# First MoE layer norm: the variance on all partitions, and its Newton steps on 256 columns

## The chip, the cores and the metric

One core of one Trainium2 chip runs the whole program. The metric is device time in microseconds (us) for one execution; a median over runs is given. The engines are TensorE (PE, with its weight loads as PEld), VectorE (DVE), ScalarE (ACT) and GpSimd (POOL); SyncE (SP) issues most transfers.

## The reference, cut to what matters

Three layers follow each other: attention with two sparse masks (4 batches of 576 tokens, 8 heads of 64), a first MoE layer on the 2304 tokens of 512 features, and a second MoE layer with eight experts. The change concerns the layer norm at the head of the first MoE:

```
mu = mean(x); var = mean((x - mu) ** 2)           # over the 512 features of a token
xn = (x - mu) / sqrt(var + 1e-6) * g_ln
x  = x + relu(xn @ w_ch1) @ w_ch2                 # 512 -> 2048 -> 512
```

## The kernel before, in words

Tokens are cut into nine chunks of 256 (CT); features lie on the partitions, so a chunk x is a tile of 128 x 4 x 256 and a mean over features is a product with `mean_w`, a 128 x 128 matrix of 1/512. Such a product leaves the mean of every token on all 128 partitions. The factor 1/sqrt(var) isn't applied to x but to the result of the second product: `post` multiplies the accumulated output by it, so it isn't needed before the chunk's last turn.

The first MoE runs in turns t. A turn is one pair (chunk c, block f of 128 hidden features): `mm1` makes 12 products into ps_h, ScalarE and VectorE split h = relu(ps_h) into a high and a low part (L641, L642), and one turn later `mm2` adds 12 products into acc. Chunks 0 and 1 are interleaved in turns 0 to 31 (chunk 0 ends in turn 28, chunk 1 in turn 31), because the weights are still being prepared there: each of 32 pieces goes through VectorE (L455), ScalarE (L461, L462), VectorE (L467, the join), ScalarE (L481, the cast to the high part) and GpSimd (L484, the low part). Attention of the next batch runs between them in turns 8 to 26 (ps_sc, sm, ps_pt, ps_o). Chunks 2 to 8 follow one by one.

Layer norm of chunks 0 and 1, by functions placed at turns through `when(t, ...)`: `ln_2` takes the mean and subtracts it, `ln_3` squares, `ln_4` takes the variance and the inverse root, `ln_back` adds the mean again, and `ln_5` brings the root into its final form. ln_4 is at turns 3 and 9, ln_5 at turns 27 and 30. In ln_4, each of two blocks of 128 tokens takes four products with one column of mean_w, the squares being the weights, so that the variance of a token stands on the token's own partition, in two columns; an integer guess and three Newton steps (three VectorE instructions each) follow on 128 x 2. ln_5 scales the identity by the two columns (dg), multiplies it by mean_w into ps_rs, and ScalarE copies the 128 x 256 result to rsb. Chunks 2 to 8 already use `ln_w`, which works on 128 x 256 after one product.

Instructions are written in this order, but a scheduler puts each engine's queue in order beforehand: of the instructions that are ready by its own clock it takes the one written first, so that one written late can stand early in a queue. Instructions marked with `keep` (those of the weight pieces) stay in order among themselves. On the chip each queue runs in its fixed order.

Buffers: pools with a tag have as many buffers as `bufs`; ln_p has one each of the tags sq, mu, rs and s, and a new tile of a tag waits for the last reader of the old one. side_r gives one of two PSUM buffers in this stage.

Of the kernel before, what the change touches and what calls it, by code (L numbers as in the profile page):

```python
# [9 lines left out]
F32 = mybir.dt.float32  # L10
# [3 lines left out]
I32 = mybir.dt.int32  # L14
U32 = mybir.dt.uint32
AF = mybir.ActivationFunctionType
ALU = mybir.AluOpType
# [6 lines left out]
DM, DF = 512, 2048  # L24
# [4 lines left out]
CT = 256  # L29
NCHUNK = NT // CT  # L30
TT = 128
NTT = CT // TT
# [40 lines left out]
def attention_moe_moe(ctx: ExitStack, tc: tile.TileContext, q, k, v, g_ln, w_ch1, w_ch2, w_gate, w_local, w1, w2, out):  # L73
# [15 lines left out]
    pe, act, dve = Pin(nc.tensor), Pin(nc.scalar), Pin(nc.vector)  # L89
# [14 lines left out]
    ident = iw[:, 0, NE + 1:NE + 129]  # L104
    make_identity(nc, ident)
    pool.tensor_copy(iw[:, 1, NE + 1:NE + 129], ident)
    mean_w = cst.tile([128, 128], F32, name="mean_w")
# [46 lines left out]
    rt_p = ctx.enter_context(tc.tile_pool(name="rt_p", bufs=1))  # L154
    ps_acc = ctx.enter_context(tc.tile_pool(name="ps_acc", bufs=1, space=PSUM))
    ps_m = ctx.enter_context(tc.tile_pool(name="ps_m", bufs=2, space=PSUM))

    at_x = ExitStack()
    at_p = at_x.enter_context(tc.tile_pool(name="at_p", bufs=1))
# [19 lines left out]
    def side_r(shape, name):  # L179
        return ps_s["r"].tile(shape, F32, tag="s", name=name)  # L180
# [373 lines left out]
    def ln_3(c):  # L554
# [11 lines left out]
            pool.tensor_tensor(s_, s_, sq, op=ALU.add)  # L566
        lns[c] = s_

    def ln_4(c):

        s_ = lns[c]
        ps = side_r([128, NTT], "ps_var")
        for j in range(NTT):
            for d in range(4):
                pe.matmul(ps[:, j:j + 1], s_[:, d, TT * j:TT * j + TT], mean_w[:, 0:1], start=(d == 0), stop=(d == 3))
        va = ln_p.tile([128, 3, NTT], F32, tag="va", bufs=2, name="va")
        va, rs, t = (va[:, i, :] for i in range(3))
        dve.tensor_scalar(va, ps, 1e-6, None, op0=ALU.add)
        dve.tensor_single_scalar(rs.bitcast(I32), va.bitcast(I32), 1, op=ALU.logical_shift_right)
        dve.tensor_scalar(rs.bitcast(I32), rs.bitcast(I32), -1.0, float(0x5F3759DF), op0=ALU.mult, op1=ALU.add)  # L580
        for _ in range(3):
            dve.tensor_tensor(t, rs, rs, op=ALU.mult)
            dve.scalar_tensor_tensor(t, t, -0.5, va, op0=ALU.mult, op1=ALU.mult)
            dve.scalar_tensor_tensor(rs, t, 1.5, rs, op0=ALU.add, op1=ALU.mult)
        lns[c] = rs

    newton = {}

    def ln_w(c, k):

        if k == 0:
            ps = side_r([128, CT], "ps_var")
            pe.matmul(ps, mean_w, lns[c], start=True, stop=True)
            va, t, rs = (ln_p.tile([128, CT], F32, tag=g, name=n) for g, n in (("sq", "va"), ("mu", "nt"), ("rs", "rsb")))
            newton[c] = va, t
            lns[c] = rs
            dve.tensor_scalar(va, ps, 1e-6, None, op0=ALU.add)
            dve.tensor_single_scalar(rs.bitcast(I32), va.bitcast(I32), 1, op=ALU.logical_shift_right)
            dve.tensor_scalar(rs.bitcast(I32), rs.bitcast(I32), -1.0, float(0x5F3759DF), op0=ALU.mult, op1=ALU.add)
        else:  # L600
            va, t = newton[c]
            rs = lns[c]
            dve.tensor_tensor(t, rs, rs, op=ALU.mult)
            dve.scalar_tensor_tensor(t, t, -0.5, va, op0=ALU.mult, op1=ALU.mult)
            dve.scalar_tensor_tensor(rs, t, 1.5, rs, op0=ALU.add, op1=ALU.mult)

    def ln_5(c):
        rs = lns[c]
        dg = ln_p.tile([128, NTT, TT], F32, tag="sq", name="dg")
        for j in range(NTT):  # L610
            dve.tensor_scalar(dg[:, j, :], ident, rs[:, j:j + 1], float(DM), op0=ALU.mult, op1=ALU.mult)
        ps = side_r([128, CT], "ps_rs")
        pe.matmul(ps, mean_w, dg.rearrange("p j t -> p (j t)"), start=True, stop=True)
        rsb = ln_p.tile([128, CT], F32, tag="rs", name="rsb")
        act.copy(rsb, ps)
        lns[c] = rsb

    def ln_split(c):
        x = xts[c]
# [347 lines left out]
    for n in range(2):  # L967
        i = n * (NE + 129)
# [49 lines left out]
    def when(t, fn, *args):  # L1018
        at.setdefault(t, []).append(lambda: fn(*args))
# [7 lines left out]
    for c in range(NCHUNK):  # L1027
        first = order.index((c, 0))
        if c > 1:
            for t, fn in zip(LN_AT if c > 2 else (-3, -2, -1), (ln_1, ln_2, ln_3)):  # L1030
                when(first + t, fn, c)
            when(first - 1, ln_split, c)
            when(first - 1, ln_back, c)
            for i, t in enumerate(LN_W):
                when(first + t, ln_w, c, i)
        else:
            when(last[c] - 1, ln_5, c)
        if c + 1 < NCHUNK:
            t = last[max(c, 1)] + (5 if c == 1 else 0)
            for i, (fn, *args) in zip(RT[c > 1], [(rt_rows, c, 0, 0), (rt_rows, c, 0, 1), (rt_rows, c, 1, 0), (rt_rows, c, 1, 1), (rt_soft, c), (rt_scan, c), (rt_list, c), (rt_hot, c), (rt_sum, c)]):  # L1040
                when(t + i, fn, *args)
# [24 lines left out]
    for t, (c, f) in enumerate(order):  # L1066
        need = (2 * f + 4 + 2 * (f == 14) if f < 15 else len(turns)) + WA if t <= last[0] else 0
        while nw[0] < min(len(turns), max(need, W_START + int(WR * t))):
            weights_next()
        if f == 0 and c > 1:  # L1070
            products()
            if c == 2:
                side_pools(False, s=4)
            elif c == 6:
                at_x.close()
                side_pools(False, s=3, r=1)
            elif c == NCHUNK - 1:
                load_turn(0)
                m2_p = ctx.enter_context(tc.tile_pool(name="m2_p", bufs=1))
        mm1(c, f)  # L1080
        while late:
            post(late.pop(), 1)
        for kind in ORDER:
            if kind == "T":
                while len(fifo["t"]) > (TL if plan.get(t) or plan.get(t + 1) else 0):
                    do("t")
            elif kind == "B":
                carry_ += plan.get(t, 0)
                while carry_:
                    carry_ -= 1  # L1090
                    prepped = pos[0] < len(steps) and steps[pos[0]][0] == "prep"
                    begin([])
                    if prepped:
                        break
            elif kind == "X":
                do_all("x")
            elif kind == "A":
                for fn in at.get(t, []):
                    fn()
            elif kind == "M":  # L1100
                products()
                pend.append((c, f))
            elif kind == "N":
                normed = take("n", 9)
                for p in [p for un in normed for p in st_norm(*un)]:
                    p()
            elif kind == "O":
                if len(fifo["o"]) > 1 or not (fifo["x"] or fifo["n"] or fifo["t"] or plan.get(t + 1) or plan.get(t + 2)):
                    do_all("o")
            else:  # L1110
                fifo["t"] += normed
# [514 lines left out]
```

## Time and profile before

| | |
|---|---|
| median of 3 runs | 873.81 us (873.71 to 874.35) |
| profiled execution | 874.09 us, span 872.0 us |
| TensorE busy | 846.9 us, 97% of the span |
| VectorE, ScalarE, GpSimd busy | 460.3, 353.9, 171.6 us |
| mean granted clock of TensorE | 0.993 |

Times in the rows below count from the span's start. A busy TensorE is modelled from matmuls that overlap, so its gaps show better in the weight loads (PEld). The number in brackets behind a row is how long the engine sat idle before it and what ended that.

### The profile page before, as it was taken

To read this page: it belongs to the slowest core of one execution; us is meant where nothing else is said; L and a number is where in the kernel's file an instruction comes from. 1 tells how busy PE (TensorE), PEld (TensorE's weight loads), DVE (VectorE), ACT (ScalarE), POOL (GpSimd) and SP (SyncE) were. 2 spreads that over 40 slices of the span, in tenths; PEclk is the share of its full clock that TensorE was granted. 3 is DMA by queue.
4 is the path that set the end of the run, shared out by engine and by line. 5 is a ranking of instruction groups with operands and counts; after the bars stand their busy time and mean duration, and the time that the engine had idled before them with its cause. 6 is when DMAs were issued, how large, how long until landed. Compare 5 with 4: busy or idle time off the path is not lost. (4 is left out here: it accounts for less than half of the span.)

```text
span 872.0 us, 18871 instructions
## 1 busy us (share of the span) xinstructions
PE 846.9 (97%) x7123; PEld 753.2 (86%) x7130; DVE 460.3 (53%) x1542; ACT 353.9 (41%) x857; POOL 171.6 (20%) x257
## 2 busy tenths in 40 slices
PE   9999999999999999999999999999999999999994
PEld 5688888889999999999999999999788868778773
DVE  4876765457656546566555464585815151121641
ACT  3787876542455233354211222242113252222551
POOL 2245542240120120120111212010032122121111
PEclk9999999999999999999999999999999999999998
DMA  9936352211211102210000000501266275454830
GB/s 181 263 122 207 100 150 70 52 32 53 66 44 45 50 9 59 52 32 15 26 2 26 1 26 1 194 30 45 89 240 235 70 257 207 147 186 170 300 121 23
DMA packets 96547, 87.16 MB, mean 100 GB/s; under 512 B 67379, under 2 KB 75575, under 8 KB 96441
## 3 DMA queue, kind: packets, MB, share of 16 engines
q1 hardware_dynamic: 89256, 69.61, 26.6%
q0 software_dynamic: 3552, 11.11, 3.7%
q10 hardware_dynamic: 3632, 5.09, 1.6%
q8 instruction: 59, 0.97, 0.4%
q14 instruction: 48, 0.39, 0.1%
HBM read 76.27 MB, written 9.97 MB: 99 GB/s over the span
## 5 line engine op out<-in xcount | busy, mean ns | idle before, releaser
L655 PE MATMUL acc<-h,w 128*128 128x256 f32 x1728 | 246.2, 290 | 3.2 <-DVE h L642 1.8
L639 PE MATMUL ps_h<-xc,w 128*128 128x256 f32 x1728 | 236.8, 286 | 0.0
L655 PEld LDWEIGHTS acc<-h,w 128*128 128x128 f32 x1728 | 218.5, 191 | 9.6 <-DVE h L642 3.1
L639 PEld LDWEIGHTS ps_h<-xc,w 128*128 128x128 f32 x1728 | 219.3, 192 | 1.7
L641 ACT ACTIVATE h<-ps_h 128x256 fp32r<-128x256 f32 x144 | 55.7, 388 | 214.4 <-PE ps_h L639 200.0
L642 DVE SCALAR_TENSOR_TENSOR h<-ps_h,h 128x256 fp32r<-128x256 f32 x144 | 60.4, 420 | 100.8 <-ACT h L641 100.4
L87 PE MATMUL ps_y<-wx,ht 128*128 128x512 f32 x336 | 83.6, 398 | 0.0
L484 POOL TENSOR_TENSOR w<-stg,w 128x128 fp32r<-128x128 f32 x128 | 62.9, 523 | 104.1 <-ACT w L481 54.5
L87 PE MATMUL ps_h<-wx,xs 128*128 128x512 f32 x336 | 81.0, 397 | 0.0
L87 PEld LDWEIGHTS ps_h<-wx,xs 128*128 128x128 f32 x336 | 62.7, 188 | 14.8
L87 PEld LDWEIGHTS ps_y<-wx,ht 128*128 128x128 f32 x336 | 61.1, 188 | 11.9 <-issue 0.2
L896 DVE TENSOR_TENSOR xs<-ps_tx,xs 128x512 fp32r<-128x512 f32 x14 | 9.7, 692 | 63.5 <-ACTq L1369 47.9
L1461 ACT ACTIVATE h<-ps_h 128x512 f32<-128x512 f32 x28 | 15.2, 595 | 56.4 <-PE ps_h L87 56.4
L785 DVE TENSOR_TENSOR wx<-raw,wx 128x1024 fp32r<-128x1024 f32 x32 | 37.3, 1217 | 1.3 <-ACT wx L782 1.3
L461 ACT ACTIVATE stg<-stg 128x512 f16<-128x512 f32 x27 | 37.1, 1374 | 0.3 <-DVE stg L455 0.3
L1475 DVE TENSOR_TENSOR ht<-ps_th,ht 128x512 fp32r<-128x512 f32 x28 | 18.5, 685 | 32.9 <-ACT ht L1474 32.8
L1499 POOL DMA_INDIRECT out_dram<-y,idx x14 | 17.8, 1270 | 89.7 <-ACT y L1498 81.0
L782 ACT CAST wx<-raw 128x1024 fp32r<-128x1024 f32 x32 | 31.8, 1059 | 5.6 <-PE acc L655 4.1
L355 ACT ACTIVATE sm<-sm,st 128x54 f32<-128x54 f32 (+1 forms) x80 | 27.6, 348 | 12.7 <-DVE st L343 12.6
L1474 ACT CAST ht<-ps_th 128x512 fp32r<-128x512 f32 x28 | 15.1, 589 | 36.2 <-PE ps_th L87 36.2
L467 DVE SCALAR_TENSOR_TENSOR stg<-stg 128x512 int32<-128x512 int32 x27 | 18.9, 700 | 16.4 <-ACT stg L462 15.6
L875 POOL DMA_INDIRECT xg<-xrows,idx x15 | 16.1, 1073 | 54.1 <-issue 33.1
(397 smaller groups left out, 1181.5 us busy)
## 6 DMA issues: line engine op xcount, KB each, us to landing
raws<-in_moe_w_dram SPq DMA_DIRECT2D x20, 1024.0 KB
stg<-in_moe_w_ch_dram SPq DMA_DIRECT2D x32, 512.0 KB
raw<-in_moe_w_dram SPq DMA_DIRECT2D x16, 1024.0 KB
xrows<-row ACTq DMA_DIRECT2D x9, 520.0 KB
qnat<-in_q_dram SPq DMA_DIRECT2D x48, 72.0 KB
knat<-in_k_dram SPq DMA_DIRECT2D x48, 72.0 KB
v<-in_v_dram SPq DMA_DIRECT2D x24, 72.0 KB
v<-in_v_dram SPq DMA_DIRECT2D x72, 18.0 KB
```

The lines of the kernel that those rows point to most:

```text
L87: return lambda *args, **kw: tc.keep_in_program_order(fn(*args, **kw))
L355: act.activation(sm[0:m, i, :], (ps if mode else sm)[0:m, i, :], AF.Exp, bias=st[0:m, 0, i:i + 1], scale=-1.0, **({} if mode else dict(acc ...
L461: keep(act.activation(t.bitcast(F16)[..., 1], f32(t[..., 1]), AF.Copy, scale=2.0 ** -112))
L467: keep(dve.scalar_tensor_tensor(t[..., 1], t[..., 1], 3, t[..., 0], op0=ALU.logical_shift_left, op1=ALU.bitwise_or))
L484: keep(pool.tensor_tensor(o, x, f32(h), op=ALU.subtract))
L639: pe.matmul(ps, w[:, a, d, o:o + 128], xcs[c][:, b_, d, :], start=(i == 0), stop=(i == 11))
L641: act.activation(h[:, 0, :], ps, AF.Relu)
L642: dve.scalar_tensor_tensor(h[:, 1, :], ps, 0.0, f32(h[:, 0, :]), op0=ALU.max, op1=ALU.subtract)
L655: pe.matmul(accs[c][d // 2][:, d % 2, :], w[:, a, f % 2, d * 128:(d + 1) * 128], h[:, b_, :], start=(f == 0 and (a, b_) == (0, 0) and d % ...
L782: act.copy(wx[i][:, 0, :], raw[i // 2][:, i % 2, :])
L785: dve.tensor_tensor(wx[i][:, 1, :], raw[i // 2][:, i % 2, :], f32(wx[i][:, 0, :]), op=ALU.subtract)
L1475: dve.tensor_tensor(s_[1][:, 4 * g:4 * g + 4, :], ps, f32(s_[0][:, 4 * g:4 * g + 4, :]), op=ALU.subtract)
```

## The change: what it does

For chunks 0 and 1 the variance is taken as the mean is: four products of 256 columns with mean_w as weights, which leaves it on all partitions as 128 x 256. Only the addition of 1e-6 stays in ln_4. The integer guess and the three Newton steps work on 128 x 256 and are placed at the four turns 24 to 27 (chunk 0) and 27 to 30 (chunk 1). The scaling of the identity, the product into ps_rs and ScalarE's copy go. Chunk 1 gets a buffer of its own for va, in a pool that is closed after turn 31, and a tag of its own, rs1, for the result. `ln_w` of the later chunks calls the same helpers and does what it did.

```diff
+    va_x = ExitStack()
+    va_p = va_x.enter_context(tc.tile_pool(name="va_p", bufs=1, side="right"))
...
     def ln_4(c):
-        s_ = lns[c]
-        ps = side_r([128, NTT], "ps_var")
-        for j in range(NTT):
-            for d in range(4):
-                pe.matmul(ps[:, j:j + 1], s_[:, d, TT * j:TT * j + TT], mean_w[:, 0:1], start=(d == 0), stop=(d == 3))
-        va = ln_p.tile([128, 3, NTT], F32, tag="va", bufs=2, name="va")
-        va, rs, t = (va[:, i, :] for i in range(3))
+        ps = side_r([128, CT], "ps_var")
+        for d in range(4):
+            pe.matmul(ps, mean_w, lns[c][:, d, :], start=(d == 0), stop=(d == 3))
+        va = (va_p if c else ln_p).tile([128, CT], F32, tag="sq", name="va")
         dve.tensor_scalar(va, ps, 1e-6, None, op0=ALU.add)
+        newton[c] = va, None
+
+    def ln_5(c, k):
+        if k == 0:
+            newton[c] = va, t = newton[c][0], ln_p.tile([128, CT], F32, tag="mu", name="nt")
+            lns[c] = ln_p.tile([128, CT], F32, tag=("rs", "rs1")[c], name="rsb")
+            seed(c)
+        else:
+            newton_step(c)
+
+    def seed(c):
+        va, rs = newton[c][0], lns[c]
         dve.tensor_single_scalar(rs.bitcast(I32), va.bitcast(I32), 1, op=ALU.logical_shift_right)
         dve.tensor_scalar(rs.bitcast(I32), rs.bitcast(I32), -1.0, float(0x5F3759DF), op0=ALU.mult, op1=ALU.add)
-        for _ in range(3):
-            dve.tensor_tensor(t, rs, rs, op=ALU.mult)
-            dve.scalar_tensor_tensor(t, t, -0.5, va, op0=ALU.mult, op1=ALU.mult)
-            dve.scalar_tensor_tensor(rs, t, 1.5, rs, op0=ALU.add, op1=ALU.mult)
-        lns[c] = rs
+
+    def newton_step(c):
+        (va, t), rs = newton[c], lns[c]
+        dve.tensor_tensor(t, rs, rs, op=ALU.mult)
+        dve.scalar_tensor_tensor(t, t, -0.5, va, op0=ALU.mult, op1=ALU.mult)
+        dve.scalar_tensor_tensor(rs, t, 1.5, rs, op0=ALU.add, op1=ALU.mult)
...
-    def ln_5(c):
-        rs = lns[c]
-        dg = ln_p.tile([128, NTT, TT], F32, tag="sq", name="dg")
-        for j in range(NTT):
-            dve.tensor_scalar(dg[:, j, :], ident, rs[:, j:j + 1], float(DM), op0=ALU.mult, op1=ALU.mult)
-        ps = side_r([128, CT], "ps_rs")
-        pe.matmul(ps, mean_w, dg.rearrange("p j t -> p (j t)"), start=True, stop=True)
-        rsb = ln_p.tile([128, CT], F32, tag="rs", name="rsb")
-        act.copy(rsb, ps)
-        lns[c] = rsb
...
-            when(last[c] - 1, ln_5, c)
+            for i in range(4):
+                when(last[c] - 4 + i, ln_5, c, i)
...
+        if t == last[1]:
+            va_x.close()
```

## Rows read from the trace of the kernel before

**Rows 1.** Busy time by stage (instructions in brackets), then clock, DMA share, GB/s.

```profile
57.00:87.00 30.00, 28.52 (x238) 27.13 (x236) 21.73 (x51) 24.59 (x39) 17.18 (x32) 1.00 0.50 154
87.00:105.00 18.00, 16.67 (x134) 15.29 (x133) 13.77 (x43) 15.14 (x24) 9.18 (x20) 0.91 0.32 108
...
160.00:177.00 17.00, 16.40 (x167) 14.66 (x164) 6.29 (x20) 8.20 (x22) 5.16 (x11) 1.00 0.14 31
...
195.00:605.00 410.00, 409.33 (x3804) 395.37 (x3802) 243.86 (x934) 138.24 (x453) 50.50 (x47) 1.00 0.15 41
```

**Rows 2.** Waits of 85.9 to 105: us in total, times, longest.

```profile
DVE stg L467 <- ACT stg L462: 3.3, 2, 2.8
...
ACT w L481 <- DVE stg L467: 1.5, 3, 0.8
```

**Rows 3.** Timeline, weight loads: mean of chunk 1, variance of chunk 1.

```profile
55.14 1.17 PEld L545 LDWEIGHTS ps_mu<-xt,mean_w 128*128 128x128 f32 x6
...
86.58 1.86 PEld L575 LDWEIGHTS ps_var<-mean_w,sq 128*128 128x128 f32 x16
```

**Rows 4.** Timeline, 69 to 74, first and last of eight short steps among them.

```profile
69.03 0.67 ACT L481 CAST w<-stg 128x512 fp32r<-128x512 f32 x1 [0.51 <-DVE stg L467]
69.53 0.15 DVE L583 SCALAR_TENSOR_TENSOR va<-va 128x2 f32<-128x2 f32 x1
...
70.71 0.48 ACT L641 ACTIVATE h<-ps_h 128x256 fp32r<-128x256 f32 x1
70.72 0.40 DVE L584 SCALAR_TENSOR_TENSOR va<-va 128x2 f32<-128x2 f32 x1
...
71.77 0.16 DVE L584 SCALAR_TENSOR_TENSOR va<-va 128x2 f32<-128x2 f32 x1
...
72.19 0.42 DVE L642 SCALAR_TENSOR_TENSOR h<-ps_h,h 128x256 fp32r<-128x256 f32 x1
...
72.65 1.37 PEld L655 LDWEIGHTS acc<-h,w 128*128 128x128 f32 x11 [1.11 <-DVE h L642]
...
73.23 0.67 ACT L481 CAST w<-stg 128x512 fp32r<-128x512 f32 x1 [1.50 <-DVE stg L467]
```

**Rows 5.** Timeline, 94 to 106, first and last of nine short steps among them.

```profile
94.01 0.15 DVE L582 TENSOR_TENSOR va<-va 128x2 f32<-128x2 f32 x1
94.08 0.45 DVE L367 TENSOR_REDUCE st<-sm 128x3 f32<-128x288 f32 x1
...
98.38 0.15 DVE L584 SCALAR_TENSOR_TENSOR va<-va 128x2 f32<-128x2 f32 x1
...
105.43 0.28 PEld L280 LDWEIGHTS ps_tr<-iw,qnat 96*128 96x128 f32 x3 [1.56 <-ACT pt L383]
```

**Rows 6.** Instructions on tile va: ns min/median/max, first and last start.

```profile
L604 DVE SCALAR_TENSOR_TENSOR nt<-nt,va x21: 417/425/427, 200.7 to 555.4; 128x256 f32<-128x256 f32 x21
...
L598 DVE TENSOR_SCALAR rsb<-va x7: 293/294/297, 199.5 to 551.2; 128x256 int32<-128x256 int32 x7
```

**Rows 7.** Timeline, weight loads, 173 to 187.

```profile
174.11 0.31 PEld L613 LDWEIGHTS ps_rs<-dg,mean_w 128*128 128x128 f32 x2
174.45 0.41 PEld L639 LDWEIGHTS ps_h<-xc,w 128*128 128x128 f32 x2
...
182.93 0.30 PEld L613 LDWEIGHTS ps_rs<-dg,mean_w 128*128 128x128 f32 x2
...
186.04 1.14 PEld L655 LDWEIGHTS acc<-h,w 128*128 128x128 f32 x9 [1.10 <-ACT w L481]
```

**Rows 8.** Timeline, VectorE, 73 to 79.

```profile
73.12 0.48 DVE L611 TENSOR_SCALAR dg<-iw,va 128x128 f32<-128x128 f32 x2
...
78.90 0.42 DVE L642 SCALAR_TENSOR_TENSOR h<-ps_h,h 128x256 fp32r<-128x256 f32 x1 [1.89 <-ACT h L641]
```

**Rows 9.** Busy time by stage, as in rows 1, around the products of chunk 1.

```profile
86.60:88.40 1.80, 1.80 (x19) 1.80 (x17) 0.63 (x1) 1.08 (x2) 0.35 (x1) 1.00 0.97 316
...
89.40:92.80 3.40, 3.40 (x18) 3.40 (x17) 2.77 (x8) 2.87 (x5) 1.72 (x5) 0.52 0.77 261
```

More of the change, by code (lines that the diff above doesn't have):

```diff
@@ L567, in ln_3 @@
         lns[c] = s_
+    newton = {}
     def ln_4(c):
-        s_ = lns[c]
-        ps = side_r([128, NTT], "ps_var")
-        for j in range(NTT):
-            for d in range(4):
-                pe.matmul(ps[:, j:j + 1], s_[:, d, TT * j:TT * j + TT], mean_w[:, 0:1], start=(d == 0), stop=(d == 3))
-        va = ln_p.tile([128, 3, NTT], F32, tag="va", bufs=2, name="va")
-        va, rs, t = (va[:, i, :] for i in range(3))
-        dve.tensor_scalar(va, ps, 1e-6, None, op0=ALU.add)
+        ps = side_r([128, CT], "ps_var")
+        for d in range(4):
+            pe.matmul(ps, mean_w, lns[c][:, d, :], start=(d == 0), stop=(d == 3))
+        va = (va_p if c else ln_p).tile([128, CT], F32, tag="sq", name="va")
+        dve.tensor_scalar(va, ps, 1e-6, None, op0=ALU.add)
+        newton[c] = va, None
[8 more added lines that the diff above has]
+        va, rs = newton[c][0], lns[c]
         dve.tensor_single_scalar(rs.bitcast(I32), va.bitcast(I32), 1, op=ALU.logical_shift_right)
         dve.tensor_scalar(rs.bitcast(I32), rs.bitcast(I32), -1.0, float(0x5F3759DF), op0=ALU.mult, op1=ALU.add)
-        for _ in range(3):
-            dve.tensor_tensor(t, rs, rs, op=ALU.mult)
-            dve.scalar_tensor_tensor(t, t, -0.5, va, op0=ALU.mult, op1=ALU.mult)
-            dve.scalar_tensor_tensor(rs, t, 1.5, rs, op0=ALU.add, op1=ALU.mult)
-        lns[c] = rs
-    newton = {}
+    def newton_step(c):
[3 more added lines that the diff above has]
+        dve.scalar_tensor_tensor(rs, t, 1.5, rs, op0=ALU.add, op1=ALU.mult)
     def ln_w(c, k):
@@ L597, in ln_w @@
             dve.tensor_scalar(va, ps, 1e-6, None, op0=ALU.add)
-            dve.tensor_single_scalar(rs.bitcast(I32), va.bitcast(I32), 1, op=ALU.logical_shift_right)
-            dve.tensor_scalar(rs.bitcast(I32), rs.bitcast(I32), -1.0, float(0x5F3759DF), op0=ALU.mult, op1=ALU.add)
-        else:
-            va, t = newton[c]
-            rs = lns[c]
-            dve.tensor_tensor(t, rs, rs, op=ALU.mult)
-            dve.scalar_tensor_tensor(t, t, -0.5, va, op0=ALU.mult, op1=ALU.mult)
-            dve.scalar_tensor_tensor(rs, t, 1.5, rs, op0=ALU.add, op1=ALU.mult)
-    def ln_5(c):
-        rs = lns[c]
-        dg = ln_p.tile([128, NTT, TT], F32, tag="sq", name="dg")
-        for j in range(NTT):
-            dve.tensor_scalar(dg[:, j, :], ident, rs[:, j:j + 1], float(DM), op0=ALU.mult, op1=ALU.mult)
-        ps = side_r([128, CT], "ps_rs")
-        pe.matmul(ps, mean_w, dg.rearrange("p j t -> p (j t)"), start=True, stop=True)
-        rsb = ln_p.tile([128, CT], F32, tag="rs", name="rsb")
-        act.copy(rsb, ps)
-        lns[c] = rsb
+            seed(c)
+        else:
+            newton_step(c)
     def ln_split(c):
```

## Prediction

> **What bounds the kernel now.** I began with busy time by stage [rows 1]: from 195 to 605 us TensorE is busy 409.33 of 410 us, so there the end moves only with TensorE's own work, and the edit has none there. What the edit touches lies before 195, where TensorE has gaps: 16.67 of 18 us in 87 to 105, and the clock row of that stretch is 0.91. Next the waits of 85.9 to 105 [rows 2]: the long ones run in a circle, VectorE's join of a weight piece (L467) waits for ScalarE's L462, ScalarE's cast (L481) waits for L467, and nothing outside TensorE waits for TensorE. TensorE stands still for VectorE. So up to 105 us the ScalarE-VectorE loop over the weight pieces sets the pace. Then the timelines of each place at which the old steps ran: the products of the variance, the Newton steps, the row broadcast.
>
> **Products of the variance.** Removed: per chunk 16 weight loads with a one-column product each, 1.86 us [rows 3], 0.116 us apiece. Added: four f32 products of 256 columns with mean_w as weights, two loads each. The nearest row is the mean of chunk 1 with the same operands: six loads in 1.17 us, 0.195 each [rows 3]; eight make 1.56. TensorE saves 0.30 us per chunk. But both places lie in the stretch where TensorE waits later anyway [rows 2]: chunk 0's products run before the stall at 72.65 [rows 4], chunk 1's before the one at 105.43 [rows 5]. I count 0 of 0.60; 0.60 is the other bound.
>
> **Newton steps taken out of turns 3 and 9.** Chunk 0's steps of two columns fill VectorE from 69.53 to 71.93 with eight instructions; four of them take 0.35 to 0.40 us where the others take 0.15 [rows 4]. Behind them stand L455, then the split of h (L642, started 72.19), then L467. ScalarE's part of h had started at 70.71 and took 0.48, so the split is 1.0 us late; TensorE then stood 1.11 us and ScalarE 1.50 us before its next cast [rows 4]. The loop's turns before and after take about 3.5 us from cast to cast and this one 4.20 (69.03 to 73.23), so the loop lost 0.7. What is late next without it is the loop itself. Gain 0 to 0.7; I take 0.4, because wide instructions may be put into the same hole (below).
>
> Chunk 1's steps: nine more short ones from 94.01 to 98.38 [rows 5], each moving the next start by 0.07 us (94.01 to 94.08 is the first). VectorE works nearly without a gap there and ScalarE waits for it [rows 2]; TensorE's loads then wait 1.56 us for ScalarE at 105.43 [rows 5]. Taking them out gives 9 x 0.07 = 0.6 us on that chain. I count 0.6. The sum va = variance + 1e-6 stays at its turn, now 256 columns wide: 0.42 us, taken from the other wide steps [rows 6], for 0.15. Chunk 1's stands before a wait of VectorE for ScalarE in the same loop, which covers 0.27; without that cover it costs 0.27.
>
> **Broadcast of the result taken out (old ln_5).** Per chunk two scalings of the identity on VectorE, one f32 product, one copy on ScalarE. The product delays TensorE from 174.11 to 174.45 and 182.93 to 183.27, 0.34 us each [rows 7]. At 174 nothing else holds TensorE, and behind the product stands the last attention output, whose copies come before the cast that starts the last weight pieces; so 0.34 counts, and the chain of weights behind it moves along. The second is followed by the stall at 186.04, 1.10 us for ScalarE's cast [rows 7], which ends when the weight piece ends: 0 counted, 0.34 the other bound. The copies on ScalarE had waits around them: 0.
>
> **Newton steps put in on 256 columns.** Per chunk two integer instructions at 0.29 and nine at 0.42 [rows 6]: 4.4 us, 8.7 for both. Where they run is the open point. The program asks for turns 24 to 27 and 27 to 30, some 161 to 184 us, where VectorE is busy 6.29 of 17 us [rows 1]. But the order on an engine isn't the program's: the old scaling dg of chunk 0, asked for at turn 27, ran at 73.12 [rows 8], as soon as its input existed and VectorE seemed free. I expect the same here: chunk 0's steps from about 67 us on (their buffer rs holds chunk 1's mean until ln_back of turn 5 has read it), chunk 1's after those, in holes. In the loop's turns VectorE idles ahead of h, 1.89 us at 78.90 [rows 8], room for four or five; so most cost nothing. What hides them is that idle time; an instruction that lands just ahead of a waiting h or L467 costs up to 0.42. From nothing to all 22 in the way (9 us) are the ends; I take none beyond the 0.3 us that I held back at 72 us.
>
> On these instructions a rule speaks against the change. Row first: the short steps took 0.40 instead of 0.15 while GpSimd was subtracting weight pieces [rows 4], 0.25 more. The Trainium skill, SBUF — State Buffer, "SBUF: two separate sides", says that a VectorE instruction with two SBUF inputs and a GpSimd instruction lock each other out of a shared port pair for a whole instruction. All nine steps have two SBUF inputs, and the trace agrees with the rule in direction. It is the mechanism of the third rival below; the forecast doesn't use it.
>
> **Sum.** 0.4 + 0.6 + 0.34 = 1.34, with bounds: 0.6 + 0.7 + 0.6 + 0.68 = 2.6 gained at best without the clock, nothing gained at worst, and the wide instructions' cost. The profiled execution took 874.09 us (span 872.0 and 2.09 around it); 874.09 - 1.34 = 872.75. The median of the runs lies 0.28 below that execution, so 872.4 as a median. A measurement of this kernel can't tell 0.2%, 1.75 us, from no change.
>
> **Rivals.**
> First, the clock counts. Before 88.4 TensorE ran chunk 1's one-column products for 1.8 us, and from 89.4 to 92.8 its granted clock reads 0.52, which is the 1.2 GHz level for nearly all of it [rows 9]. 3.40 x 0.48 = 1.6 us of TensorE time. With 256-column products in that place the fall may not come. The Trainium skill, TensorE: Matmul & The Clock Gate, Part 1, has the gate set by how busy the array has lately been; the fall behind thin products agrees. Against it, the stretch with chunk 0's products, 57 to 87, has a clock of 1.00 throughout [rows 1]. For it to reach the end TensorE must be what holds the stretch, and rows 2 speak against it. If it does: 872.4 - 1.6 = 870.8.
>
> Second, nothing arrives. Either the hole at 69.5 to 71.9 is refilled and the other gains go into the waits at 105.43 and 186.04, or chunk 1's steps stay at turn 30: the mean of chunk 2 takes the buffer mu that they use, so ScalarE's copy of it, and the cast queued behind it, wait for the last step, 3 x 0.42 = 1.27 us on the chain that ends the stall at 186.04. Time 873.8, or 873.7 with the wait and 1.3 gained.
>
> Third, slower: the wide instructions go into VectorE's queue between 66 and 105 us ahead of h or L467, where the loop is the pace. Each moves the start behind it by 0.34 us free, by 0.6 when GpSimd holds it (0.34 + 0.25). Four undo the gain; it is slower by over 0.2% from ten of the 22, or from six at 0.6. With ten, 3.4 us: 872.4 + 3.4 = 875.8. For it speaks that the scheduler placed short ones just so at 72 us; against it, that the steps now have the lowest rank of all that is ready, and that the old ones had nearly the first.
>
> **How the numbers follow.** Forecast 0.42, clock 0.25, nothing 0.15, slower 0.18. The forecast's own range, with the bounds of its terms, is 871.2 to 873.8; some 0.12 of its 0.42 lies beyond 1.75 us of gain. So faster 0.25 + 0.12 = 0.37, same 0.30 + 0.15 = 0.45, slower 0.18. The range for 8 in 10 reaches down beyond the clock's 870.8, to 870.2, and up to 875.4, short of the ten instructions of the third rival.
>
> **What would show it.** In the changed trace: eight loads for ps_var in some 1.6 us twice and none for ps_rs; no short VectorE steps around 70 and 96; the cast after 69 us within 3.6 of the one before it, and the one around 101 us earlier by 1; the wide steps in idle time of VectorE, chunk 0's soon after 67; the granted clock 1.00 through 89 to 93, with a longer stall of TensorE by 105. The stall at 186 about as long as now. I am wrong if wide steps stand ahead of h with TensorE waiting, if the stall at 105 grows or goes by reordering that has nothing to do with these instructions, or if the stretch after 195 differs in length by more than 0.3 us.

## The result, and the profile after

The changed kernel takes 882.69 us in the median (878.91 to 884.25, 5 runs) against 874.28 (873.71 to 876.28, 5 runs) of the kernel before: 8.4 us between the medians. The ratio of the runs is 1.0080, 95% interval 1.0062 to 1.0098, or 7.0 us (5.4 to 8.6) slower. The prediction was 872.4 us, with 875.4 as its upper end. The profiled execution took 882.92 us, span 881.0, 9.0 more than before. Lines have moved: ps_h is L637, h L639 and L640, the weight pieces L458, L464, L465, L470, L484 and L487, ps_tr L283, qT L296, the Newton steps L599 to L601.

Busy time by stage in the changed kernel, columns as in [rows 1]; the last two rows are short stretches to which I come below:

```profile
57.00:87.00 30.00, 26.30 (x193) 23.81 (x192) 24.01 (x47) 25.12 (x39) 18.85 (x32) 1.00 0.15 50
87.00:105.00 18.00, 15.93 (x124) 14.69 (x125) 11.29 (x29) 12.51 (x20) 7.49 (x16) 0.81 0.58 186
105.00:130.00 25.00, 22.19 (x219) 20.35 (x218) 17.50 (x47) 16.02 (x30) 8.51 (x17) 0.93 0.36 105
195.00:605.00 410.00, 408.40 (x3788) 393.56 (x3787) 244.43 (x938) 139.77 (x459) 55.08 (x53) 1.00 0.15 41
...
89.60:93.50 3.90, 3.90 (x21) 3.67 (x19) 1.52 (x4) 2.83 (x5) 1.73 (x4) 0.50 0.17 38
112.00:114.00 2.00, 2.00 (x11) 2.00 (x11) 0.37 (x2) 1.97 (x3) 1.69 (x4) 0.50 0.55 126
```

Against [rows 1] TensorE is busy 2.2 us less in 57 to 87, and its clock in 87 to 105 is 0.81 where it was 0.91. The steady stretch after 195 is what it was, to a microsecond. So nearly all of the loss is where the edit works, ahead of 130 us. (The DMA share moves too, from 0.50 to 0.15 and from 0.32 to 0.58, since q, k and the weight pieces are fetched at other times; but no engine waits for a transfer between 55 and 125 us.) The weight loads of TensorE there, in the timeline of the changed kernel:

```profile
57.04 0.74 PEld L578 LDWEIGHTS ps_var<-sq,mean_w 128*128 128x128 f32 x4
58.17 1.25 PEld L653 LDWEIGHTS acc<-h,w 128*128 128x128 f32 x10 [0.40 <-DVE h L640]
...
64.67 0.74 PEld L578 LDWEIGHTS ps_var<-sq,mean_w 128*128 128x128 f32 x4
...
83.06 0.58 PEld L283 LDWEIGHTS ps_tr<-iw,qnat 96*128 96x128 f32 x6
...
89.07 0.45 PEld L283 LDWEIGHTS ps_tr<-iw,knat 96*128 96x128 f32 x3 [3.71 <-ACT qT L296]
...
89.67 2.68 PEld L637 LDWEIGHTS ps_h<-xc,w 128*128 128x128 f32 x12
...
94.59 1.59 PEld L578 LDWEIGHTS ps_var<-sq,mean_w 128*128 128x128 f32 x8 [0.16 <-issue]
...
110.76 0.29 PEld L283 LDWEIGHTS ps_tr<-iw,qnat 96*128 96x128 f32 x3 [2.19 <-ACT pt L386]
...
112.14 2.68 PEld L637 LDWEIGHTS ps_h<-xc,w 128*128 128x128 f32 x12
...
194.06 1.45 PEld L653 LDWEIGHTS acc<-h,w 128*128 128x128 f32 x10 [1.22 <-ACT w L484]
```

and the same queue of the kernel before, at two places that the prediction didn't look at:

```profile
58.62 0.37 PEld L280 LDWEIGHTS ps_tr<-iw,qnat 96*128 96x128 f32 x3
58.94 1.26 PEld L655 LDWEIGHTS acc<-h,w 128*128 128x128 f32 x10
...
64.84 0.33 PEld L280 LDWEIGHTS ps_tr<-iw,qnat 96*128 96x128 f32 x3
```

There the six transposes of q for the next attention unit (b = 1, hp = 0; its `prep` is written in turn 8) stood early, in two gaps of TensorE at 58.6 and 64.8. Now the two halves of chunk 0's products stand at these places, and the q transposes come in one block at 83.06. On the chip there would have been room for three of them behind the first half: TensorE idles 0.40 us there and goes on at 58.17, where the kernel before went on at 58.94. The order was made beforehand, by the scheduler's own estimates, which no trace shows. The q transposes fill both side_r buffers, and the k transposes behind them wait until ScalarE has copied qT out. ScalarE does its weight piece first (timeline of the changed kernel, ScalarE):

```profile
86.89 0.65 ACT L484 CAST w<-stg 128x512 fp32r<-128x512 f32 x1 [0.54 <-DVE stg L470]
87.45 1.33 ACT L464 ACTIVATE stg<-stg 128x512 f16<-128x512 f32 x1
88.54 0.48 ACT L296 ACTIVATE qT<-ps_tr 128x288 f32<-128x288 f32 x1
```

TensorE stands still for 3.71 us and then runs at half its clock: 0.50 from 89.6 to 93.5, the 1.2 GHz level (the short stretches of the first fence). The same happens, shorter, at 110.76, and the clock is 0.50 from 112 to 114. A ps_h block takes 2.68 us there and 1.51 elsewhere. VectorE, in the changed kernel's timeline, shows where the wide steps went:

```profile
72.69 0.41 DVE L640 SCALAR_TENSOR_TENSOR h<-ps_h,h 128x256 fp32r<-128x256 f32 x1
73.03 0.28 DVE L594 TENSOR_SCALAR rsb<-va 128x256 int32<-128x256 int32 x1
...
73.67 0.63 DVE L599 TENSOR_TENSOR nt<-rsb 128x256 f32<-128x256 f32 x1
74.33 0.57 DVE L600 SCALAR_TENSOR_TENSOR nt<-nt,va 128x256 f32<-128x256 f32 x1
74.94 0.57 DVE L601 SCALAR_TENSOR_TENSOR rsb<-nt,rsb 128x256 f32<-128x256 f32 x1
75.51 0.88 DVE L470 SCALAR_TENSOR_TENSOR stg<-stg 128x512 int32<-128x512 int32 x1
...
108.14 0.42 DVE L600 SCALAR_TENSOR_TENSOR nt<-nt,va 128x256 f32<-128x256 f32 x1
108.47 0.43 DVE L365 TENSOR_SCALAR st<-st 128x3 f32<-128x3 f32 x1
108.82 0.41 DVE L601 SCALAR_TENSOR_TENSOR rsb<-nt,rsb 128x256 f32<-128x256 f32 x1
...
109.35 0.52 DVE L367 TENSOR_TENSOR sm<-sm,st 128x288 f32<-128x288 f32 x1
```

Five of chunk 0's wide instructions stand in a row ahead of the join L470 at 75.51, which they hardly hold up, since ScalarE's L465 that it needs ended at 75.47; the last ones of chunk 1 alternate with the softmax of the attention unit (L365, L367) just ahead of the standstill at 110.76.

To compare stages I use one table. It gives how much later than in the profiled kernel before five marks come in each profile: the same ps_h block (124.34 us before), the first product of chunk 2's variance (198.38), that of chunk 8 (549.75), the first transpose of the second MoE that waits for its gather (642.48) and the next but one group of them (654.06). The last columns are the medians and the ratio's interval, each against runs of the kernel before made beside it. A row's marks are those of one execution, and executions of one kernel differ (878.91 to 884.25 for the changed kernel), so a difference of a us between two rows is no proof by itself. Labels are those of the experiments below.

```
kernel                     124   198   550   642   654   median  ratio (95%)
after                     +8.0  +7.2  +7.7  +9.0  +9.0   882.69  1.0062-1.0098
e1  q late, before        +3.0  +3.0  +3.1  +3.1  +3.1   877.16  1.0014-1.0041
e2  extra products, bef.  +5.9  +5.9  +5.9  +5.6  +5.6   879.74  1.0037-1.0080
e3  q first               +4.4  +3.7  +4.1  +4.8  +4.8   878.87  1.0034-1.0067
e4  steps late            +4.2  +6.7  +7.3  +8.0  +9.6   882.71  1.0059-1.0107
e5  steps mid             +4.8  +5.3  +6.0  +7.4  +9.0   881.67  1.0055-1.0091
e6  q first, steps mid    +3.2  +5.3  +6.2  +7.5  +9.1   880.97  1.0056-1.0084
e7  q first, before       +2.6  +2.5  +2.5  +2.3  +2.3   875.94  1.0006-1.0026
e8  q first, steps late   +3.3  +5.9  +6.9  +8.2  +9.8   882.02  1.0058-1.0096
e9  no steps              +4.4  +4.0  +4.6  +6.9  +6.9   881.42  1.0045-1.0084
e10 q first, no steps     +5.0  +4.6  +4.7  +5.2  +6.8   880.64  1.0038-1.0077
e11 extra steps, before   +0.7  +0.7  +1.4  +1.7  +1.7   877.06  1.0013-1.0034
e12 short steps late, bef.+0.7  +0.9  +0.9  +1.2  +2.8   874.26  0.9982-1.0000
e13 products late         +3.8  +4.1  +4.2  +5.3  +5.3   881.29  1.0049-1.0089
e14 products late, before +1.8  +1.8  +1.8  +0.9  +0.9   876.12  1.0004-1.0028
e15 products late, no st. +4.3  +3.9  +4.7  +5.1  +5.1   879.64  1.0035-1.0067
e16 products late, st. mid+3.1  +3.6  +4.6  +5.0  +5.0   879.90  1.0036-1.0078
e17 one product, no steps +1.6  +1.3  +1.4  +0.9  +0.9     -
e18 e17, products late    +1.2  +0.9  +1.3  +1.0  +1.0     -
```

### The profile page after: what moved, and what is told of

Read it like the earlier page. It is cut to its first block, busy times and chain, and to the rows that moved or that the text cites. A ratio compares the mean times of both kernels' runs of the same rounds, so it can differ in the third digit from the quotient of the medians.

```text
span 881.0 us, 18831 instructions
## 1 busy us (share of the span) xinstructions
PE 849.7 (96%) x7103; PEld 754.1 (86%) x7110; DVE 464.7 (53%) x1538; ACT 354.8 (40%) x855; POOL 173.8 (20%) x257
## 5 line engine op out<-in xcount | busy, mean ns | idle before, releaser
L637 PE MATMUL ps_h<-xc,w 128*128 128x256 f32 x1728 | 237.8, 287 | 0.3 <-DVE xc L621 0.3
L637 PEld LDWEIGHTS ps_h<-xc,w 128*128 128x128 f32 x1728 | 220.5, 193 | 2.3 <-DVE xc L621 0.7
L639 ACT ACTIVATE h<-ps_h 128x256 fp32r<-128x256 f32 x144 | 55.1, 383 | 216.0 <-PE ps_h L637 200.6
L640 DVE SCALAR_TENSOR_TENSOR h<-ps_h,h 128x256 fp32r<-128x256 f32 x144 | 60.3, 419 | 94.3 <-ACT h L639 94.0
L487 POOL TENSOR_TENSOR w<-stg,w 128x128 fp32r<-128x128 f32 x128 | 65.0, 538 | 109.9 <-ACT w L484 70.8
L464 ACT ACTIVATE stg<-stg 128x512 f16<-128x512 f32 x27 | 37.1, 1374 | 0.9 <-DVE stg L458 0.9
L470 DVE SCALAR_TENSOR_TENSOR stg<-stg 128x512 int32<-128x512 int32 x27 | 19.8, 732 | 19.3 <-ACT stg L465 18.8
```

Of the source, the lines that this page charges most:

```text
L464: keep(act.activation(t.bitcast(F16)[..., 1], f32(t[..., 1]), AF.Copy, scale=2.0 ** -112))
L470: keep(dve.scalar_tensor_tensor(t[..., 1], t[..., 1], 3, t[..., 0], op0=ALU.logical_shift_left, op1=ALU.bitwise_or))
L487: keep(pool.tensor_tensor(o, x, f32(h), op=ALU.subtract))
L637: pe.matmul(ps, w[:, a, d, o:o + 128], xcs[c][:, b_, d, :], start=(i == 0), stop=(i == 11))
L639: act.activation(h[:, 0, :], ps, AF.Relu)
L640: dve.scalar_tensor_tensor(h[:, 1, :], ps, 0.0, f32(h[:, 0, :]), op0=ALU.max, op1=ALU.subtract)
```

## The experiments

Each round sets theories against each other; a theory goes when a run misses the time that it gave. Most of them go, and what is left stands at the end.

**First four: two theories.** Theory one: the products take the two gaps from the q transposes (above). Theory two: the wide steps ahead of h, the join and the softmax. e1 and e2 put each side of theory one into the kernel before; e3 and e4 take one suspect each out of the changed kernel.

e1, in `prep` of the kernel before: the q transposes of that unit are held behind the last instruction that TensorE was given (`behind_now`, used below too, issues behind the last instruction written for an engine).

```diff
+            with behind_now(ET.PE) if (b, hp, nm) == (1, 0, "q") else ExitStack():
                 pe.transpose(ps[:, QT * i:QT * i + QT], ...)
```

> The kernel before, with one thing changed: the six transposes of q of the first unit of batch 1 stay behind what the program writes ahead of them on TensorE, so that they can't fill gaps 25 us early. Products, Newton steps and the broadcast are the old ones. Theory one (the lost gaps: the wide products take the places of these transposes, which then come in one block, fill both side PSUM buffers and wait for ScalarE's copies): 878 to 882 us, TensorE standing 3 us or more ahead of the transposes of k, a clock of 0.5 behind it. Theory two (the wide Newton steps hold up h and the weight pieces on VectorE): 874, no such wait.

877.16, outside both expectations. The transposes came in one block at 82.67, the k transposes waited 2.81 us for qT, and 3.0 us were lost by 124 us. The direction is theory one's; the size is less than half of the change's.

e2, in ln_4 of the kernel before: four products that nothing reads, beside its own.

```diff
-        ps = side_r([128, NTT], "ps_var")
+        ps_ = side_r([128, NTT + CT], "ps_var")
+        for d in range(4):
+            pe.matmul(ps_[:, NTT:], mean_w, s_[:, d, :], start=(d == 0), stop=(d == 3))
+        ps = ps_[:, 0:NTT]
```

> The kernel before, with the four wide products of 256 columns made as well as the 16 of one column, into columns of the same tile that nobody reads; Newton steps and broadcast as before. Theory one: the transposes are pushed back by the products alone, 878 to 883 us (the products' own 1.6 us per chunk included). Theory two: 874 to 876, no more than the products' own time.

879.74, in theory one's range. The q transposes were pushed to 82.84 and the wait was 4.18 us, as in the changed kernel, without a single wide step (TensorE's loads in e2):

```profile
89.63 0.28 PEld L280 LDWEIGHTS ps_tr<-iw,knat 96*128 96x128 f32 x3 [4.18 <-ACT qT L293]
```

But this kernel also does 3.1 us more on TensorE (two groups of 1.5 and 1.6), of the 5.9 that it is late by 124.

e3, the changed kernel with q loaded at turn 1 and transposed at turn 2.

```diff
-    when(LB, load_qk, *pairs[4])
+    when(1, load_qk, *pairs[4])
+    when(2, prep, *pairs[4], "q")
```

> The changed kernel, with loads and transposes of q of the first unit of batch 1 written at turns 1 and 2, ahead of the variance of chunk 0, so that they rank before its products. Theory one: the wait of 3.7 us at 89 and the clock's fall behind it go, 874 to 876 us. Theory two: 881 to 883, as the Newton steps stand where they stood.

878.87: between the two. The wait at 89 is gone, but two others have come, for the scores' sum on VectorE, the second behind wide instructions (from 95.22 on), the first with none ahead of it (timeline, TensorE's loads):

```profile
94.40 0.10 PEld L322 LDWEIGHTS <-iw 128*128 128x128 bf16 x1 [1.59 <-DVE sm L342]
100.52 0.10 PEld L322 LDWEIGHTS <-iw 128*128 128x128 bf16 x1 [2.04 <-DVE sm L342]
```

e4, the changed kernel with the integer instructions and steps held at the turns that the program names, 24 to 30.

```diff
     def ln_5(c, k):
+        with behind_now(ET.DVE):
+            ln_5_(c, k)
```

> The changed kernel, with the wide seed and Newton steps held behind what the program writes ahead of them on VectorE, so that they run at turns 24 to 30 and not from 73 us on. Theory one: 880 to 882 us; only the 1 us that chunk 0's steps cost between 73 and 81 comes back, the wait at 89 stays. Theory two: 873 to 875.

882.71, no gain; theory two alone falls. The table shows why no gain: by 124 us 3.8 of the 8.0 us are saved, by 198 all but 0.5 of that is lost, where chunk 2's subtraction stands behind the steps, and ScalarE's copy of its mean waits for the last of them (0.57 us, L552 for L611 at 196.63; they share the buffer mu):

```profile
199.19 0.30 PEld L647 LDWEIGHTS ps_h<-xc,w 128*128 128x128 f32 x2 [1.64 <-ACT xc L630]
```

**Next four: do the two add?** Theory three: gaps 4 us, steps 4 us, separate. Theory four: the steps cost wherever VectorE does them. The steps go to turns 16 to 23, `when((16, 20)[c] + i, ln_5, c, i)` with the hold of e4 (e5), also with the q transposes first (e6); e7 puts the q transposes first in the kernel before; e8 joins e3 and e4.

> The changed kernel with the wide Newton steps held at turns 16 to 19 and 20 to 23, behind what VectorE was given before, so between the stretch of 73 to 130 us and the start of chunk 2. Theory three (two separate losses: the gaps that the products take from the q transposes, 4 us, which the run with the steps held to turns 24 to 30 still showed at 125 us; and the steps ahead of the weight pieces and the softmax, 4 us more, which that run had saved by 125 us and lost again at chunk 2's start): 877 to 879, that is 4 us over the kernel before, with the wait at 89 us still there and none of the new waits at 199 us. Rival, theory four (the wide steps cost their time wherever VectorE does them, as work on a loaded engine): 881 to 883, as with the steps at either end.

> The changed kernel with both: the q transposes of the late unit written at turn 2 ahead of the products, and the wide steps held at turns 16 to 23. Theory three (two separate losses that add): both are gone, 873 to 875.5, level with the kernel before. Rival, theory four (the steps cost their time anywhere): 878 to 880, as with the q transposes first alone.

> The kernel before with the q transposes of the late unit written at turn 2 (and loaded at turn 1) as in the variants above, nothing else. Theory three: in the kernel before they stand in those gaps already, so 873.5 to 875, the same. Rival (moving the transposes forward is a gain of its own, and what the changed kernel won back by it was no loss of the change): 870 to 872, some 3 us faster than the kernel before.

> The changed kernel with the q transposes first and the wide steps held at the turns that the program names, 24 to 30. Theory three: nothing lost up to 190 us, then the wait at chunk 2's start behind the last steps, 2 to 4 us: 876 to 878.5. Rival, theory four (the steps cost the same anywhere): 878 to 880, and a loss that is already there before 190 us.

881.67, 880.97, 875.94, 882.02. Theory three falls: e6 has neither of its losses and is 5 to 7 us slower. Its trace has a wait of 2.76 us for the scores' sum (sm, L342) at 100.71 instead. e5 at 124 us is as e4 there (+4.8 and +4.2). e7 missed both expectations: nothing is added, one preparation comes earlier, and 2.5 us are gone by 198. Theory four's numbers fit e5 alone.

**Products or steps.** Theory five: both cost. Theory six: it is the products and the order that comes with them. e9 drops the Newton steps of the changed kernel (`newton_step(c)` out of ln_5), e10 with the q transposes first; e11 adds the wide instructions to the kernel before, where TensorE's order stays; e12 holds the old kernel's own short steps at turns 16 and 20.

> The changed kernel with the Newton steps of chunks 0 and 1 left out (18 of the 22 wide VectorE instructions; the two integer instructions of each chunk stay, so the result is the rough first value). What is left of the change is the products. Theory five (both parts cost: the products 4 to 5 us through the q transposes, the steps 2 to 4 us more wherever they stand): 878 to 880, with the wait at 89 us as in the changed kernel and no wait for VectorE behind it. Rival, theory six (the products and the new order that they bring are all of it, and the steps only seemed to matter by changing the order again): 881 to 883.

> The same, with the q transposes of the late unit written at turn 2 ahead of the products: neither the lost gaps nor the steps. Theory five: level with the kernel before that has its q transposes first, 875 to 876.5. Theory six: 878 to 881, as the other variants with the q transposes first.

> The kernel before with the 22 wide VectorE instructions beside what it does, on data that nothing reads (one sum and four integer instructions and 18 steps, in all 23 with the sum), asked for at turns 24 to 30 as in the change and taken early by the scheduler as there; TensorE's order up to the k transposes is that of the kernel before. Theory five: 2 to 4 us slower, 876.5 to 878.5, with TensorE waiting for h and for the softmax between 73 and 110 us. Theory six: within 1 us, 874 to 876, as VectorE has the time.

> The kernel before with its own short Newton steps, on two columns, held at turns 16 and 20 in place of turns 3 and 9; products, broadcast and all else as before. It takes out of the weight loop just what the change took out, and puts nothing wide in. The prediction's step (0.4 us at 70 us and 0.6 us at 96 us gained): 873.5 to 874.2, with the cast behind 69 us 0.7 us earlier. Rival (that time isn't on the path that sets the end, or the order that the scheduler makes of it eats it): 874.5 to 877.

881.42, 880.64, 877.06, 874.26. In e9 the wait at 89 us is 4.17 and the loss at 124 us 4.4, as in e4 and e5: with the steps absent, late or in the middle, what the products bring is 4.2 to 4.8 us by then. The median is theory six's, 2.4 us of it after 550. The second standstill is short (TensorE's loads in e9):

```profile
89.37 0.28 PEld L283 LDWEIGHTS ps_tr<-iw,knat 96*128 96x128 f32 x3 [4.17 <-ACT qT L296]
...
108.56 0.28 PEld L283 LDWEIGHTS ps_tr<-iw,qnat 96*128 96x128 f32 x3 [1.28 <-ACT pt L386]
```

(1.28, with 1.22 in e1 and 1.56 in [rows 5], against 2.19 in the changed kernel.) In these profiles the early steps cost 3.2 to 3.8 us by 124 us in the changed kernel's order. Against e9 the difference is 0.9 us at the ps_h block that started at 99.67 in the kernel before, and 3.3 at the one of 111.19: most of it falls at the second standstill and the half clock behind it. In the medians little of it is left: 882.69 with the steps, 881.42 without, with intervals that overlap.

In the kernel before's order, e11, as many wide instructions cost 0.7 us by 124 and 2.4 us in the median (874.61 beside it), as theory five had it; its longest wait there is 1.44 us, at 97.45 for the softmax (L367). It isn't quite the same test: both chunks' steps read one tile that is there from 69.5 on, so all of them had run by 93, and none stood among the softmax of 97 to 109, as chunk 1's do in the changed kernel.

e10 goes against theory five: its q transposes are early, it has no steps, and it is 5.0 us behind at 124; theory six had its time.

e12 shows where a gain goes. The short steps are gone from VectorE, and the block that follows the old hole starts 5.82 us after the block two before it, where it took 6.92 (67.03 to 73.95): 1.1 us gained. TensorE's loads in e12:

```profile
67.53 1.51 PEld L654 LDWEIGHTS ps_h<-xc,w 128*128 128x128 f32 x12
...
71.85 1.57 PEld L670 LDWEIGHTS acc<-h,w 128*128 128x128 f32 x12
73.35 1.51 PEld L654 LDWEIGHTS ps_h<-xc,w 128*128 128x128 f32 x12
...
87.30 2.58 PEld L580 LDWEIGHTS ps_var<-mean_w,sq 128*128 128x128 f32 x16 [1.20 <-DVE kT L289]
89.76 2.68 PEld L670 LDWEIGHTS acc<-h,w 128*128 128x128 f32 x12
92.32 2.68 PEld L654 LDWEIGHTS ps_h<-xc,w 128*128 128x128 f32 x12
```

The wait of 1.11 us [rows 4] is gone; at 87.30 a new one of 1.20 stands, the clock falls behind it, and the block that was at 90.21 is at 92.32. That is the profiled execution, which took 876.61 us. The median is 874.26 beside 874.61, and the ratio's interval of 0.9982 to 1.0000 allows anything from no gain to 1.6 us: whether the 1.0 us that the prediction counted stays, these runs don't tell.

**Products behind the transposes.** Theory seven: the two gaps, plus 2 us for steps. Chunk 0's products go to turn 9 and chunk 1's to turn 14, so that the transposes have both gaps: q in the first, half of k in the second.

```diff
-LN01, LN_AT, LN_W = (1, 1, 3, 1, 1, 4, 5, 9), (-7, -5, -4), (1, 2, 3, 4)
+LN01, LN_AT, LN_W = (1, 1, 9, 1, 1, 10, 11, 14), (-7, -5, -4), (1, 2, 3, 4)
```

e13 is the changed kernel so, e14 the kernel before so, e15 is e13 without the steps, e16 is e13 with the steps as in e5.

> The changed kernel with the products of chunk 0 at turn 9 and those of chunk 1 at turn 14 (turns 3 and 9 in the change; the squares of chunk 1 and the sum that restores it go to turns 10 and 11 behind them). In TensorE's order the transposes of the late unit then stand in the two gaps, six of q in the first and three of k in the second, and the products follow behind the first scores, some 95 us. Theory seven (the loss is the two gaps, plus some 2 us for the wide steps): the wait of 4 us at 89 us and the clock's fall behind it are gone, at most 2 us behind the kernel before at 198 us, 875.5 to 878. Theory six (products and a new order cost wherever they stand): 879 to 882.

> The kernel before with the same turns (its one-column products and short steps of chunk 0 at turn 9, of chunk 1 at turn 14). Control for the moved turns. Theory seven: the gaps are now all the transposes', so level or a little faster, 872.5 to 875. Theory six (any other order than the one before costs 2 us or more): 876 to 878.

> The changed kernel with the products at turns 9 and 14 and the 18 wide Newton steps left out (the rough first value stays). Products alone, behind the transposes. Theory seven: level with the kernel before, 873 to 875.5, against 881.4 with the products in the gaps. Theory six: 878 to 881.

> The changed kernel with the products at turns 9 and 14 and the wide steps held at turns 16 to 19 and 20 to 23. Theory seven: the gaps are kept and the steps are out of the weight loop's stretch, 874 to 877, not slower than with the steps left to the scheduler. Rival (VectorE's 8.7 us cost the same wherever they stand): 2 us over the run without steps, 876 to 878.5. Theory six: 879 to 882.

881.29, 876.12, 879.64, 879.90: theory six's numbers in all four. Theory seven falls: e15, with the gaps kept for the transposes and no steps, is at +4.3. And here the early steps cost next to nothing: e13, which has them, is 0.5 us ahead of e15 at 124 and 0.7 behind e16. With the q transposes first it is the same: e3 is 0.6 us ahead of e10, and 1.1 to 1.2 behind e6 and e8. e14 and e15 are the cleanest pair. Both start chunk 0's products in the same place, and the wide ones are shorter. TensorE's loads in e15, then in e14:

```profile
86.09 1.59 PEld L578 LDWEIGHTS ps_var<-sq,mean_w 128*128 128x128 f32 x8
...
99.54 0.11 PEld L322 LDWEIGHTS <-iw 128*128 128x128 bf16 x1 [2.45 <-DVE sm L342]
```

```profile
86.19 1.86 PEld L575 LDWEIGHTS ps_var<-mean_w,sq 128*128 128x128 f32 x16
```

e15 also has less on VectorE (no steps) and no row broadcast. Yet its ScalarE squares chunk 1 at 92.72, behind a weight piece, where e14's did so at 89.70. And its VectorE puts a whole weight piece ahead of the sum of the next scores (L342), which e14's takes at 96.07, ahead of the softmax's end (e15, VectorE):

```profile
96.24 0.52 DVE L367 TENSOR_TENSOR sm<-sm,st 128x288 f32<-128x288 f32 x1
96.68 0.68 DVE L458 TENSOR_SCALAR stg<-stg 128x512 int32<-128x512 int32 x1
97.29 0.68 DVE L470 SCALAR_TENSOR_TENSOR stg<-stg 128x512 int32<-128x512 int32 x1
97.89 0.41 DVE L458 TENSOR_SCALAR stg<-stg 128x512 int32<-128x512 int32 x1
98.22 0.41 DVE L638 SCALAR_TENSOR_TENSOR h<-ps_h,h 128x256 fp32r<-128x256 f32 x1
98.56 0.44 DVE L340 TENSOR_REDUCE st<-ps_sc 128x3 f32<-128x288 f32 x1
99.03 0.46 DVE L342 TENSOR_TENSOR sm<-ps_sc,st 128x288 f32<-128x288 f32 x1
```

TensorE waits 2.45 us for it at 99.54, and its clock then reads 0.50 from 99.90 to 105. Up to the ps_h block that started at 95.15 in the kernel before, e15 was 1.1 us ahead of that kernel; one block on it is 3.9 behind. Less work on TensorE and VectorE, and 2.5 us later by 124: what differs for the worse is the order of the queues, made beforehand.

**Is it the products' room?** Theory eight: the room of four products. Theory nine: the rest of the change. e17 is e9 and e18 is e15 with `for d in range(4)` cut to d = 0. With that variance other tokens go to other experts and the second MoE does more tiles, so these two are read to 654 us only.

> As the run without the Newton steps, and of the four products of each chunk only the first is made (the variance lacks three quarters of its sum). In TensorE's order the q transposes then stand in the two gaps, behind one product, as in the kernel before. Theory eight (what costs is the room that the four products take on TensorE): 873 to 876, level with the kernel before, against 881.4 with four. Rival, theory nine (it is the rest of the change, and the order of VectorE and ScalarE that follows from it): 878 to 881.

> As the run with the products at turns 9 and 14 and without the Newton steps, and only the first of the four products of each chunk is made; TensorE's order is else the same. Theory eight: the three products left out are some 1.2 us of TensorE per chunk, 875 to 878. Theory nine: as with four, 878.5 to 880.5, with the wait for the scores' sum on VectorE still there at about 97 to 100 us.

The whole times (915.07, 913.41) say nothing for that reason. At 124 us e17 is at +1.6 against +4.4, e18 at +1.2 against +4.3: 2.8 and 3.1 us less, for 6 x 0.4 = 2.4 us of loads left out (1.59 us hold four products). In e17 the q transposes stand in the two gaps again (TensorE's loads):

```profile
57.28 0.44 PEld L283 LDWEIGHTS ps_tr<-iw,qnat 96*128 96x128 f32 x3
...
64.86 0.33 PEld L283 LDWEIGHTS ps_tr<-iw,qnat 96*128 96x128 f32 x3
```

That is for theory eight against nine. The wait for the scores' sum, which theory nine named, is there all the same: 2.62 us at 98.10 in e17, 0.96 at 99.23 in e18. And e17 does 3.1 us less on TensorE than the kernel before (0.3 against 1.86 per chunk) and is still 1.6 us behind it: the room is bought back about one for one, and the order stays the worse one.

## Why the prediction was wrong, point by point

**The step that failed** is the first term, the products: "both places lie in the stretch where TensorE waits later anyway. I count 0 of 0.60". The durations were right (1.59 against 1.86 on the chip, 1.56 against 1.86 predicted). What I didn't price is that the scheduler makes the queues anew around a product of another shape. In the changed kernel it put the products into gaps in which other work stood, and this moved a block of transposes to where ScalarE is late; with that block elsewhere, other waits took its place. By 124 us this is 4.2 to 4.8 us of the 8.0 (e4, e5, e9), and 3.1 to 5.0 in the other arrangements without early steps (e6, e8, e10, e15, e16). I looked at what waits behind the products in the old order, not at what stands in the gaps that the new ones would fit.

**The wide steps** went where I expected, from about 73 us on, but not into idle time. The third rival came nearest, with ten of the 22 in the way, 3.4 us: the profiles show 3.2 to 3.8 by 124 us in this kernel (after against e4, e5, e9). That the price fits is in part luck. It was counted for steps ahead of h or the join; most of it fell at the softmax, as a longer standstill and the clock behind it. And it belongs to this order alone: in the other orders the early steps cost -0.6 to 1.2 us (e3 against e6, e8, e10; e13 against e15, e16), and 0.7 in e11. I gave this rival 0.18 and a time of 875.8, since it stood alone there, without the products. The Trainium skill's rule behind it (SBUF — State Buffer, "SBUF: two separate sides", a mutual lock of VectorE and GpSimd) agrees with the trace again: steps that take 0.41 to 0.43 us alone took 0.57 and 0.63 at 73.67 to 75.51, while GpSimd worked on a weight piece. The second rival's wait, of chunk 2's mean for the last step, didn't come here, since the steps ran early; it came where they were held to turns 24 to 30, in e4.

**Short steps taken out**: at 70 us the gain is real, 1.1 us in e12 against 0.4 counted, and in e12's profile it is given back at 87 to 92. "What is late next without it is the loop itself" was wrong there: next was a transpose's copy, and the clock. In the changed kernel neither part of the 1.0 us shows: the blocks that took 6.92 us take 7.17 (67.29 to 74.46), and the stall of 1.56 at 105.43 has become the 2.19 at 110.76.

**The broadcast taken out** was right. At the ps_h block that started at 174.45, right behind the old product [rows 7], the shift falls by 0.33 us in the changed kernel (7.69 to 7.36), e9 (4.42 to 4.09), e5, e13 and e16, and not in e2, e11 and e14, which keep the broadcast; 0.34 was counted. The wait for the last weight pieces is 1.22 us at 194.06 where it was 1.10 [rows 7], as forecast.

**The clock** as a rival had the wrong sign. The fall behind the one-column products [rows 9] doesn't come behind the wide ones at 94.59, but two falls come behind standstills. The Trainium skill, TensorE: Matmul & The Clock Gate, Part 1, has the gate halve the clock after the array has been idle. These falls agree with it in direction, while 1.28 us (e9) and 2.33 us (the changed kernel, below) were waits without a fall. The prediction used that page for a gain alone.

**After 195** I wrote that a difference over 0.3 us would show me wrong. It is 0.4 by 550 and 1.3 more by 642, 0.8 of it a longer wait of TensorE for the gather (PE lines of before, then of the changed kernel):

```profile
642.48 0.66 PE L882 MATMUL ps_tx<-iw,xg 128*128 128x128 f32 x4 [1.53 <-DMA xg<-xrows,idx]
```

```profile
651.49 0.66 PE L880 MATMUL ps_tx<-iw,xg 128*128 128x128 f32 x4 [2.33 <-DMA xg<-xrows,idx]
```

The sum for the profiled execution is then: products and their order 4.2 to 4.8, steps 3.2 to 3.8, the stretch from 124 to 198 -0.8 (0.33 of it the broadcast), later 1.8; 9.0 in all. The first two are no prices to be carried to another order.

**What stays open.** Why the scheduler's order comes out worse with wide products at every place that I tried. Its own clock isn't in the trace; the runs only show that most of the loss goes with three quarters of the products (e17, e18), and that moves which add nothing to the kernel before cost 0.9 to 3.0 us by 198 in their profiles (e1, e7, e12, e14), so that part of the 4 us may be any move's. An order of the changed kernel pinned to the old one wasn't tried. The 1.3 us at 642 aren't explained either: between 550 and 642 every kernel with the whole change, or all of it but the steps, loses something, from 0.4 us (e15, e16) to 2.4 (e9), and the variants of the kernel before lie between -0.9 (e14) and 0.3 (e11, e12). No version is clearly faster than the kernel before; e12 comes nearest.

## What to carry to other kernels

Where a scheduler orders the queues, an edit's price is not its instructions' durations: ask which gap each new instruction fits, what stands in that gap now, and where that goes. In a stretch in which three engines wait for each other in turn, a saved microsecond can be given back at the next meeting point, as in e12's profile. Before believing a cause, put it alone into the kernel before and take it alone out of the kernel after: here four tidy theories (one, three, five, seven) each fell in the runs made for them. And try it in more than one order: here the early steps cost over 3 us in one and at most 1.2 in two others.

## What the runs showed of the hardware

A standstill can cost more than its length. After waits of 3.71 and 2.19 us the granted clock read 0.50 (the 1.2 GHz level) and ps_h blocks took 2.68 us for 1.51; after the 1.28 us at 108.56 in e9 the stage 105 to 130 read 1.00.

The same wait is followed by a fall in one profile and not in another. The gather's wait was 2.33 us in the changed kernel, and 651 to 655 reads 1.00; in e5 it was 2.20:

```profile
650.00:654.00 4.00, 4.00 (x14) 3.23 (x14) 0.99 (x3) 0.59 (x1) 2.00 (x2) 0.61 0.32 89
```

The marks at 642 and 654 are 11.58 us apart without a fall and 13.2 with one: 1.6 us. It is in the profiles of e4, e5, e6, e8, e10 and e12, and so in the table between its last two columns. e12's profiled execution, with it, took 876.61 us, while its median is 874.26.
